# Block-sorted attention with a mixture of experts behind it: weights asked for in GpSimd's order, denominators by products of their own, an exchange on three queues

## The chip, the core and the metric

The kernel runs on one core of one Trainium2 chip. The core has five engines with instruction streams of their own: TensorE (PE; its weight loads stand as PEld), VectorE (DVE), ScalarE (ACT), GpSimd (POOL) and SyncE (SP). They share an on-chip memory, SBUF, of 128 partitions, and TensorE writes its results to PSUM, in banks of 128 partitions by 2 KB. Sixteen DMA engines move data between the chip's main memory and SBUF; an engine's stream asks for such a transfer and goes on. Streams wait for each other by semaphores. The metric is the device time in microseconds (us) of one execution; the data before is the median of three.

## The reference, cut to what matters

`P` is a small matrix for each of 4 batches and 8 heads, made near doubly stochastic by five rounds of row and column normalisation (Sinkhorn). It mixes the 8 blocks (96 rows of 64) of keys and of values; then each block of queries attends to its sorted block. The result, 3072 rows of 512, goes through 8 experts that are all computed for all rows and summed with weights from a second, longer Sinkhorn.

```python
for _ in range(5):
    P = np.exp(P - np.max(P, axis=-1, keepdims=True))
    P = P / (np.sum(P, axis=-1, keepdims=True) + 1e-09)
    P = P / (np.sum(P, axis=-2, keepdims=True) + 1e-09)
k_sorted = np.einsum('bhij,bhjcd->bhicd', P, k_b)   # v_sorted likewise
scores = scale * np.matmul(q_b, k_sb.transpose(0, 1, 2, 4, 3))
attn = np.exp(scores - max); attn /= attn.sum(-1)
x = np.matmul(attn, v_sb)                           # -> [3072, 512]
# P: 8 rounds of normalisation of exp(x @ w_gate)
for e in range(8):
    out += P[:, e:e+1] * (np.maximum(x @ w1[e], 0) @ w2[e])
```

## The kernel before, in words

**The whole.** Batch 0's attention runs alone (line numbers are the profile's, L1 is the first line of the kernel file). Batches 1, 2 and 3 follow, each woven with the first expert's products for the batch before it (`expert0`, L299 and L306), so that TensorE always has expert products to put between the short ones of the attention. Then come the other experts, about three quarters of the time, which the change does not touch. TensorE's and GpSimd's instructions are pinned to the order in which the program writes them (`pin`); those of the other engines are ordered by a scheduler unless pinned.

**The loads.** GpSimd asks for all loads from main memory (`load_rest` L75, `load_w1` L84, `load_w2` L89), since they turn 4-byte into 2-byte numbers on the way. It asks first for the gate's weights `wg` (L96), then for the queries, values and keys of batch 0 in halves of four heads, then for batch 1's values.

**Start of batch 0.** ScalarE and VectorE compute the Sinkhorn of `P` on 32 partitions (L111 to L124). `Prep` repeats it 16 times (L128), eight products spread it over the partitions (L352), VectorE copies the result to `Pb` (L354) and builds from `Pb` and a mask the block matrices `R` (`build_r`, L140), with which a single product sorts the values of a head (L152) or the keys (L196).

**Values and the exchange.** `sort_values` makes eight products, one a head; VectorE and ScalarE copy them by turns into `vs` (L154). There the 96 rows of a sorted block lie in 16 partitions, 6 to each. The mix needs them in 96 partitions. Eight DMAs, the exchange, carry block for block from `vs` to `vsb` (L161), by turns from SyncE and GpSimd. To each value row a column of ones is appended, so that the mix's 65th column is the softmax's denominator.

**Batch 0's attention.** Its plan is a string, each letter a step with its pair of heads: `q` turns the queries (TensorE L174, ScalarE copy L186), `k` sorts the keys (L196, VectorE copy L201), `s` makes scores (L215) and their exponentials on ScalarE (L222) into `atp`; `m` mixes: products of the exponentials with `vsb` (L232), two banks a head, the reciprocal of the 65th column (L235) and the product with it (L236), both on VectorE; `t` turns the result (L243) and copies it to `xtT` (L246, on ScalarE in batch 0); `l` makes the gate's logits from it (L257); `v` sorts two heads of batch 1's values, and its last call issues batch 1's exchange; `w` makes products that nobody reads (`warm`, L344, 512 columns each). The plan of batch 0 before:

```python
plan = ("k0 k1 w4 s0 q2 k2 w2 s1 q3 k3 w3 s2 w4 s3 w3 m0 w3 m1 t0 v0 w3 m2 t1 v0 w3 "
        "m3 t2 v0 v0 w3 t3 l0 w3 l3 v0" if first else
```

Seven PSUM banks go round among all these steps.

**The probe.** The first expert's weights are wanted only behind batch 0's attention. GpSimd copies two numbers of `vsb` (`held`, L362), which it can do only once the exchange has landed, and `issue_after` lets the requests for w1, w2 and batch 1's keys and queries follow that copy.

**Behind batch 0.** Twelve steps of `expert0` come first (8 of four products with w1, L299, then 4 half steps with w2, L306), then batch 1's attention, woven with the rest. It begins with the queries of both first pairs, for which the first halves of batch 1's queries must have landed; the third pair needs the second half.

Of the kernel before, what the change touches and what calls it, by code (L numbers as in the profile page):

```python
# [13 lines left out]
F32 = mybir.dt.float32  # L14
# [11 lines left out]
def kernel(  # L26
# [66 lines left out]
    make_identity(nc, Ibig)  # L93
    load_batch(0, [(x, l0, 4) for l0 in (0, 4) for x in "qvk"])
    wg = ones.tile([128, 4, E], BF16)
    nc.gpsimd.dma_start(out=wg, in_=moe_w_gate.rearrange("(kk k) e -> k kk e", k=128))  # L96
    load_batch(1, [("v", 0, 8)])
    mask16 = ones.tile([128, 16], F32)
# [5 lines left out]
    vsbt = [perp.tile([128, VW], BF16, name=f"vsb{n}") for n in range(2)]  # L104
    vs = vsp.tile([128, 6, 8, 65], BF16)
    nc.vector.memset(vs[:, :, :, 64:65], 1.0)

# [18 lines left out]
    Prep = perp.tile([32, 8, 8, 16], BF16)  # L126
    for eng, i0 in ((nc.vector.tensor_copy, 0), (nc.scalar.copy, 4)):
        eng(Prep[:, i0:i0 + 4], mkap(P, [P.ap[0], [8, 4], [1, 8], [0, 16]], off=i0 * 8))  # L128

# [4 lines left out]
    Rt = {}  # L134

    def build_r(bb, eng, n):

        Rt[bb] = perp.tile([128, 8, 8, 16], BF16, name=f"R{bb % 2}")
        for h in range(0, 8, n):
            ins = eng.tensor_tensor(  # L140
                out=mkap(Rt[bb], [Rt[bb].ap[0], [16, 8 * n], [1, 16]], off=h * 128),
                in0=mkap(Pb, [Pb.ap[0], [1, 8 * n], [0, 16]], off=(bb * 8 + h) * 8),
                in1=mkap(mask16, [mask16.ap[0], [0, 8 * n], [1, 16]]),
                op=ALU.mult)
            if eng is nc.gpsimd:
                pin(ins)


    def sort_values(bb, bank):
        for h in range(8):  # L150
            vps = bank([128, 384], F32)
            pin(nc.tensor.matmul(vps, Rt[bb][:, h].rearrange("p i c -> p (i c)"),  # L152
                                 vt[bb][:, h, :], start=True, stop=True))
            (nc.vector.tensor_copy if bb == 0 and h % 2 else nc.scalar.copy)(  # L154
                vs[:, :, h, 0:64], vps.rearrange("p (kk d) -> p kk d", d=64))
            if h % 2:
                yield

        for i in range(NB):
            eng = nc.gpsimd if i % 2 else nc.sync  # L160
            (pin if bb == 0 else lambda ins: ins)(eng.dma_start(  # L161
                out=mkap(vsbt[bb % 2], [[VW, 96], [1, 520]], off=i * 520),
                in_=vs[16 * i:16 * i + 16].rearrange("p kk h d -> p kk (h d)")))
# [43 lines left out]
    def scores(bb, hp, bank):  # L207

        for b in range(2):
# [10 lines left out]
            for h in range(2):  # L220
                at[bb, hp, h, b] = sp.tile([128, 4, 96], BF16, name="atp", bufs=ATP)
                nc.scalar.activation(out=at[bb, hp, h, b][0:96], in_=sps[h][0:96],  # L222
                                     func=AF.Exp, scale=scale)

    def mix(bb, hp, h, bank):
        if h == 0:
            og[bb, hp] = sp.tile([128, NB, 2, 64], BF16, name="og", bufs=2)
        for b in range(2):
            ops = bank([128, 4, 65], F32)
# [33 lines left out]
    def attention(bb, bank, values=None, warm=None):  # L263
        first = bb == 0

        def step(what, hp):
            if what == "q":
                queries(bb, hp, bank)
            elif what == "k":
                keys(bb, hp, bank)  # L270
            elif what == "s":
                scores(bb, hp, bank)
            elif what == "t":
                turn(bb, hp, bank, nc.scalar.copy if first else nc.vector.tensor_copy)
            elif what == "l":
                logits(bb, bank, (0, 1, 2) if hp == 0 else (3,))
            elif what == "v":
                next(values, 0)
            elif what == "w":
                warm(hp)  # L280
            else:
# [53 lines left out]
    with tc.tile_pool(name="ps0", bufs=7, space=bass.MemoryType.PSUM,  # L335
# [15 lines left out]
        for i in range(8):  # L351
            pin(nc.tensor.matmul(pbps[:, i, :], Prep[:, i].rearrange("p j c -> p (j c)"),  # L352
                                 Ibig[0:32, 0:32], start=True, stop=True))
        nc.vector.tensor_copy(Pb, pbps.rearrange("p i g -> p g i"))  # L354
# [25 lines left out]
    with ExitStack() as c2:  # L380
# [4 lines left out]
        for bb in range(1, B):  # L385
            ex = expert0(bb - 1, lambda: mps.tile([128, 8, 384], BF16, name="hTs"),
                         ebank, ebank, pin)
            at1, left = attention(bb, bank1), 16 if bb == 1 else 26
            for _ in range(28 - left):
                next(ex)  # L390
            last = 3 if bb + 1 < B else 0
            left -= last
            cut = lambda k: left * k // 12
            weave(at1, ex, 5, cut(5))
            if bb + 1 < B:
                load_batch(bb + 1, [(x, 0, 8) for x in "vkq"])
                build_r(bb + 1, nc.gpsimd, 4)
            else:
# [413 lines left out]
```

## Time and profile before

| What | us |
|---|---|
| median of 3 runs (range) | 680.86 (680.52 to 681.43) |
| profiled execution | 680.97 |
| its span | 679.2 |
| TensorE busy in the span | 659.0 |
| DMA moved | 36.58 MB, mean 54 GB/s |

The span is from the first to the last instruction of the profile; the profiled execution's own time is 1.8 us longer. A row of the timeline or of the groups reads: start, length, engine, line, operation, output `<-` inputs, shapes, how many; in brackets the idle time of the engine before it and what ended it. A matmul's shape is that of its stationary operand, then of its moving one. Neighbouring instructions of one kind are merged into one row, so that a row of 16 products holds one latency and 15 steps. A row of DMA issues reads: output `<-` input, the queue that asked (SPq, POOLq), how many, KB of each, and us from issue to landing (the median). Queue rows read: packets, MB, and the time they took as a share of 16 engines (q0 holds GpSimd's transfers, q1 SyncE's); packets overlap, so that a share can pass 100%. A row by stretches reads: from:to, length, then each engine's busy time and count (PE, PEld, DVE, ACT, POOL), the granted TensorE clock, the DMA share and GB/s.

### The profile page before, as it was taken

How to read it: one execution, taken by the hardware profiler on the slowest of the kernel's cores; microseconds unless marked ns; L12 is line 12 of the kernel's file. 1: busy time of each engine (PE TensorE's matmuls, PEld its weight loads, DVE VectorE, ACT ScalarE, POOL GpSimd, SP SyncE). 2: the span in 40 equal slices, each digit the busy share in tenths (PEclk: the TensorE clock that was granted, in tenths of full speed). 3: DMA queues.
4: the chain of work that ended last, by engine and by line, in shares of the span. 5: the costliest groups of instructions: out<-in, count | busy, mean ns of one | idle time of the engine just before them, and what ended most of it. 6: DMA issues, size and time to landing. Idle time of an engine off the chain costs nothing.

```text
span 679.2 us, 13352 instructions
## 1 busy us (share of the span) xinstructions
PE 659.0 (97%) x5136; PEld 434.1 (64%) x5136; DVE 474.8 (70%) x977; ACT 380.5 (56%) x737; POOL 473.6 (70%) x439
## 2 busy tenths in 40 slices
PE   4989999999999999999999999999999999999997
PEld 2656666554566666666666666666666666666665
DVE  6727556758587777777777777777777777777775
ACT  3757646356767765455555555555555555555540
POOL 4542324474979998959697988879796979836641
PEclk9999999999999999999999999999999999999999
DMA  9898843402140304030403030020303040000224
GB/s 146 168 217 127 139 82 63 63 1 37 28 62 2 63 1 63 1 63 1 63 1 63 1 50 14 12 52 3 61 1 63 1 63 1 1 0 32 94 84 167
DMA packets 31905, 36.58 MB, mean 54 GB/s; under 512 B 2016, under 2 KB 24288, under 8 KB 31840
## 3 DMA queue, kind: packets, MB, share of 16 engines
q0 software_dynamic: 26400, 27.82, 25.8%
q1 hardware_dynamic: 5440, 7.90, 3.4%
q8 instruction: 40, 0.66, 0.4%
q14 instruction: 25, 0.20, 0.1%
HBM read 52.45 MB, written 6.29 MB: 86 GB/s over the span
## 4 chain that ended last, share of the span: by engine, by line
PE 88%; DVE 5%; DMA 4%; issue 1%; ACT 1%; POOL 1%; SPq 0%; DVEq 0%; POOLq 0%
PE oacc L635 36%; PE bk L524 36%; PE bank L299 4%; PE bank L306 3%; DMA qt<-in_q_dram 3%; PE bank L232 1%; PE bk L601 1%; PE oacc L700 1%; PE bk L692 1%; DMA vsb<-vs 1%; PE bank L215 1%; PE bank L196 1%; PE bank L243 1%; DVE xc L460 1%; PE bk L700 1%
## 5 line engine op out<-in xcount | busy, mean ns | idle before, releaser
L585 DVE SCALAR_TENSOR_TENSOR osbl<-oacc,glog,osbl 128x256 f32<-128x256 f32 (+1 forms) x410 | 219.4, 536 | 127.7 <-PE oacc L635 117.8
L510 ACT ACTIVATE hT<-bk 128x512 bf16<-128x512 f32 (+1 forms) x176 | 104.2, 592 | 151.8 <-PE bk L524 131.9
L524 PE MATMUL bk<-xtT,w1e 128*128 128x512 bf16 x504 | 149.1, 379 | 0.0
L635 PEld LDWEIGHTS <-hs 128*128 128x128 bf16 x984 | 96.3, 98 | 63.0 <-issue 0.3
L635 PEld LDWEIGHTS <-hT 128*128 128x128 bf16 x904 | 88.4, 98 | 59.6 <-issue 2.4
L625 POOL TENSOR_TENSOR hs<-hT 128x512 bf16<-128x512 bf16 x82 | 94.7, 1155 | 38.3 <-DVE hT L513 28.6
L635 PE MATMUL oacc<-w2e,hT 128*128 128x256 bf16 x764 | 114.6, 273 | 1.1 <-DVE osbl L585 1.1
L625 POOL TENSOR_TENSOR hs<-hT,hs 128x512 bf16<-128x512 bf16 x82 | 95.1, 1159 | 6.4
L625 POOL TENSOR_TENSOR hs<-hs,hT 128x512 bf16<-128x512 bf16 x82 | 95.1, 1159 | 6.4
L524 PE MATMUL bk<-xc,wc 128*128 128x512 bf16 x336 | 99.1, 379 | 0.0
L635 PE MATMUL oacc<-w2e,hs 128*128 128x256 bf16 x616 | 92.4, 273 | 0.0
L524 PEld LDWEIGHTS <-w1e 128*128 128x128 bf16 x672 | 65.7, 98 | 14.9 <-issue 3.6
L559 ACT COPY p<-bk 128x512 f32<-128x512 f32 x84 | 49.1, 585 | 23.9 <-PE bk L524 23.8
L513 DVE CUSTOM_DVE_ANT_0 hT<-bk,p 128x512 bf16<-128x512 f32 x84 | 57.9, 690 | 6.6 <-PE bk L524 1.9
L553 ACT COPY u<-bk 128x512 f32<-128x512 f32 x84 | 49.2, 586 | 22.2 <-PE bk L524 22.1
L544 ACT COPY bk<-bk 128x512 f32<-128x512 f32 x84 | 48.0, 571 | 20.5 <-PE bk L524 20.5
L513 DVE CUSTOM_DVE_ANT_0 hT<-bk,u 128x512 bf16<-128x512 f32 x84 | 57.2, 681 | 0.6 <-PE bk L524 0.6
L635 PE MATMUL oacc<-w2s,hs 128*128 128x256 bf16 x368 | 55.2, 273 | 0.0
L578 DVE SCALAR_TENSOR_TENSOR s<-bk,hT 128x512 bf16<-128x512 f32 x80 | 54.5, 681 | 0.0
L524 PEld LDWEIGHTS <-wc 128*128 128x128 bf16 x504 | 49.4, 99 | 7.5
L524 PE MATMUL bk<-xc,w1e 128*128 128x512 bf16 x168 | 49.9, 379 | 1.9 <-DVE hT L513 1.8
L524 PE MATMUL bk<-xtT,wc 128*128 128x512 bf16 x168 | 50.0, 379 | 0.0
(129 smaller groups left out, 858.5 us busy)
## 6 DMA issues: line engine op xcount, KB each, us to landing
w1e<-in_moe_w_dram POOLq DMA_DIRECT2D x8, 1024.0 KB, 8.1
w2e<-in_moe_w_dram POOLq DMA_DIRECT2D x8, 1024.0 KB, 8.9
out_dram<-osbl SPq DMA_DIRECT2D x23, 256.0 KB, 2.0
vt<-in_v_dram POOLq DMA_DIRECT2D x3, 768.0 KB, 10.5
vsb<-vs SPq DMA_DIRECT2D x16, 97.5 KB, 4.8
vsb<-vs POOLq DMA_DIRECT2D x16, 97.5 KB, 4.4
qt<-in_q_dram POOLq DMA_DIRECT2D x4, 384.0 KB, 12.8
kt<-in_k_dram POOLq DMA_DIRECT2D x4, 384.0 KB, 13.3
```

The source lines that it names most:

```text
L299: hold(nc.tensor.matmul(hps[:, 0:n], w1t[e][:, kk, fb * 128:(fb + 1) * 128], xtT[:, kk, c0:c0 + n], start=(kk == 0), stop=(kk == 3)))
L306: hold(nc.tensor.matmul(oacc, hTs[:, fb, tt * 128:(tt + 1) * 128], w2t[e][:, fb, :], start=(fb == 0), stop=(fb == 7)))
L510: relu = lambda o, x: nc.scalar.activation(out=o, in_=x, func=AF.Relu)
L513: return nc.vector._custom_dve(TENSOR_ADD_SAT, out=o, in0=x, in1=y, s0=TOP, s1=0.0)
L524: pin(nc.tensor.matmul(ps, wa[:, kk, :], xa[:, kk, :], start=(first and kk == 0), stop=(kk == 1), skip_group_check=True))
L544: pin(nc.scalar.copy(t["w"], t["u"]))
L553: pin(nc.scalar.copy(t["u2"], t["u"]))
L559: pin(nc.scalar.copy(t["p5"], t["v"]))
L578: pin(nc.vector.scalar_tensor_tensor(out=s3[:, i, :], in0=t["w"], scalar=0.0, in1=c12, op0=ALU.max, op1=ALU.subtract))
L585: pin(nc.vector.scalar_tensor_tensor(out=o, in0=ps, scalar=glog[:, t, e:e + 1], in1=o, op0=ALU.mult, op1=ALU.add))
L625: pin(nc.gpsimd.tensor_tensor(out=s[:, c], in0=a, in1=b, op=o))
L635: pin(nc.tensor.matmul(ps, h[:, fb, :], w[:, fb, :], start=(first and fb == 0), stop=(fb == 3), skip_group_check=True))
```

## The change

What is done, part by part:

- The request for `wg` moves behind batch 1's values and is pinned there, so the loads of batch 0 are asked for first.
- `Prep` is split 5 and 3 between VectorE and ScalarE instead of 4 and 4.
- Batch 0's `R` is built by VectorE straight from the PSUM bank; `Pb` is copied by ScalarE, and its user is GpSimd's `R` of the later batches.
- Of batch 0's value copies VectorE makes those of heads 3, 5 and 7 and ScalarE the other five.
- Batch 0's exchange goes by turns from SyncE, GpSimd and ScalarE instead of SyncE and GpSimd.
- The probe copy is gone. GpSimd, behind its exchange pieces, builds half of batch 1's `R`, asks for w1, builds the other half, asks for w2 and then for batch 1's keys and queries.
- A new step `d` computes batch 0's softmax denominators by 16 products of the exponentials with a column of ones, for a pair of heads, and one reciprocal. The mix of batch 0 then has 64 columns, all eight blocks of a head in one bank, and one VectorE product of 512 elements a partition.
- The last turn's copy of batch 0 moves to VectorE.
- Heads 4 to 7 of batch 1's values, and its exchange, move from batch 0's plan to the first expert steps (`late`).
- The unread products are fewer in all (23 instead of 31) and placed anew.

```diff
     load_batch(0, [(x, l0, 4) for l0 in (0, 4) for x in "qvk"])
+    load_batch(1, [("v", 0, 8)])
     wg = ones.tile([128, 4, E], BF16)
-    nc.gpsimd.dma_start(out=wg, in_=moe_w_gate.rearrange("(kk k) e -> k kk e", k=128))
-    load_batch(1, [("v", 0, 8)])
+    pin(nc.gpsimd.dma_start(out=wg, in_=moe_w_gate.rearrange("(kk k) e -> k kk e", k=128)))
...
+    one = pp.tile([128, 1], BF16)
+    nc.vector.memset(one, 1.0)
...
-    for eng, i0 in ((nc.vector.tensor_copy, 0), (nc.scalar.copy, 4)):
-        eng(Prep[:, i0:i0 + 4], mkap(P, [P.ap[0], [8, 4], [1, 8], [0, 16]], off=i0 * 8))
+    for eng, i0, n in ((nc.vector.tensor_copy, 0, 5), (nc.scalar.copy, 5, 3)):
+        eng(Prep[:, i0:i0 + n], mkap(P, [P.ap[0], [8, n], [1, 8], [0, 16]], off=i0 * 8))
...
-    def sort_values(bb, bank):
-        for h in range(8):
+    def sort_values(bb, bank, n=8, h0=0):
+        for h in range(h0, n):
...
-            (nc.vector.tensor_copy if bb == 0 and h % 2 else nc.scalar.copy)(
+            (nc.vector.tensor_copy if bb == 0 and h in (3, 5, 7) else nc.scalar.copy)(
...
-        for i in range(NB):
-            eng = nc.gpsimd if i % 2 else nc.sync
+        for i in range(NB if n == 8 else 0):
+            eng = ((nc.sync, nc.gpsimd, nc.scalar)[i % 3] if bb == 0 else
+                   nc.gpsimd if i % 2 else nc.sync)
...
+    def denominators(hp, bank):
+
+        dps = bank([128, 2, NB], F32)
+        for h in range(2):
+            for i in range(NB):
+                pin(nc.tensor.matmul(dps[0:96, h, i:i + 1], at[0, hp, h, i // 4][0:96, i % 4, :],
+                                     one[0:96], start=True, stop=True))
+        den[hp] = pp.tile([128, 2, NB], F32, name=f"den{hp}")
+        nc.vector.reciprocal(out=den[hp][0:96], in_=dps[0:96])
...
+        if bb == 0:
+            ops = bank([128, NB, 64], F32)
+            for i in range(NB):
+                a = (i * 8 + 2 * hp + h) * 65
+                pin(nc.tensor.matmul(ops[0:96, i], at[bb, hp, h, i // 4][0:96, i % 4, :],
+                                     vsbt[0][0:96, a:a + 64], start=True, stop=True))
+            nc.vector.tensor_mul(og[bb, hp][0:96, :, h, :], ops[0:96],
+                                 mkap(den[hp], [[den[hp].ap[0][0], 96], [1, NB], [0, 64]],
+                                      off=h * NB))
+            return
...
-                turn(bb, hp, bank, nc.scalar.copy if first else nc.vector.tensor_copy)
+                turn(bb, hp, bank, nc.scalar.copy if first and hp < 3 else nc.vector.tensor_copy)
...
-        plan = ("k0 k1 w4 s0 q2 k2 w2 s1 q3 k3 w3 s2 w4 s3 w3 m0 w3 m1 t0 v0 w3 m2 t1 v0 w3 "
-                "m3 t2 v0 v0 w3 t3 l0 w3 l3 v0" if first else
+        plan = ("k0 k1 w3 s0 q2 k2 w2 s1 q3 k3 d0 w1 s2 w2 d1 s3 w7 m0 d2 w1 m1 t0 w2 m2 t1 v0 "
+                "d3 m3 t2 w2 v0 t3 l0 w3 l3" if first else
...
-        nc.vector.tensor_copy(Pb, pbps.rearrange("p i g -> p g i"))
-        build_r(0, nc.vector, 2)
+        Rt[0] = perp.tile([128, 8, 8, 16], BF16, name="R0")
+        for h in range(0, 8, 2):
+            nc.vector.tensor_tensor(
+                out=Rt[0][:, h:h + 2],
+                in0=mkap(pbps, [pbps.ap[0], [1, 2], [32, 8], [0, 16]], off=h),
+                in1=mkap(mask16, [mask16.ap[0], [0, 2], [0, 8], [1, 16]]), op=ALU.mult)
...
-        build_r(1, nc.gpsimd, 4)
-
-        held = pp.tile([96, 2], BF16)
-        gate = nc.gpsimd.tensor_copy(
-            held, mkap(vsbt[0], [[VW, 96], [520, 2]], off=6 * 520 + 519))
-        with tc.issue_after(gate.ins):
-            load_w1(0)
-            load_w2(0)
-            load_rest(1, [(x, l0, 4) for l0 in (0, 4) for x in "kq"])
-        for _ in attention(0, bank0, sort_values(1, bank0), warm):
+        nc.scalar.copy(Pb, pbps.rearrange("p i g -> p g i"))
+        half = build_r(1, nc.gpsimd, 4)
+        next(half)
+        load_w1(0)
+        next(half, 0)
+        load_w2(0)
+        load_rest(1, [(x, l0, 4) for l0 in (0, 4) for x in "kq"])
+        for _ in attention(0, bank0, sort_values(1, bank0, 4), warm):
...
+            late = sort_values(1, bank1, 8, 4) if bb == 1 else iter(())
             for _ in range(28 - left):
                 next(ex)
+                next(late, 0)
```

More of the change, by code (lines that the diff above doesn't have):

```diff
@@ L146, in build_r @@
                 pin(ins)
-    def sort_values(bb, bank):
-        for h in range(8):
+            yield
+    def sort_values(bb, bank, n=8, h0=0):
+        for h in range(h0, n):
             vps = bank([128, 384], F32)
@@ L223, in scores @@
                                      func=AF.Exp, scale=scale)
+    den = {}
+    def denominators(hp, bank):
[6 more added lines that the diff above has]
+        nc.vector.reciprocal(out=den[hp][0:96], in_=dps[0:96])
     def mix(bb, hp, h, bank):
@@ L280, in step @@
                 warm(hp)
+            elif what == "d":
+                denominators(hp, bank)
             else:
@@ L396 @@
                 load_batch(bb + 1, [(x, 0, 8) for x in "vkq"])
-                build_r(bb + 1, nc.gpsimd, 4)
+                for _ in build_r(bb + 1, nc.gpsimd, 4):
+                    pass
             else:
```

## The prediction

> **What bounds the kernel now.** I began with the page's first part and the chain of work that ended last: the profiled execution is TensorE work almost from end to end, so a change counts only where TensorE waits or is kept from starting.
>
> ```profile
> PE 659.0 (97%) x5136; PEld 434.1 (64%) x5136; DVE 474.8 (70%) x977; ACT 380.5 (56%) x737; POOL 473.6 (70%) x439
> PE 88%; DVE 5%; DMA 4%; issue 1%; ACT 1%; POOL 1%; SPq 0%; DVEq 0%; POOLq 0%
> ```
>
> Next the same chain piece by piece, up to 49 us (start, length, what), because the change touches only that part:
>
> ```profile
> 19.57 4.87 DMA vsb<-vs
> 25.06 0.83 POOL w1e L84
> 28.98 19.76 DMA qt<-in_q_dram
> 48.78 0.53 PE bank L174 x12
> ```
>
> The reader is to see a chain without TensorE: the sorted values of batch 0 set off the exchange, the exchange lands at 24.44 (19.57 + 4.87), GpSimd's probe copy then lets w1 be asked for at 25.06, and behind w1 and w2 stand the keys and queries of batch 1, whose last piece lands at 48.74. From there the chain is TensorE's. So TensorE's timeline up to that point decides (the bracket is the wait before the row):
>
> ```profile
> 18.48 0.56 PE L215 MATMUL bank<-qTs,kTs 64*96 64x96 bf16 x16 [0.44 <-DVE kTs L201]
> 23.06 1.04 PE L344 MATMUL unread<-Ibig 128*128 128x512 bf16 x4
> 24.52 0.82 PE L344 MATMUL unread<-Ibig 128*128 128x512 bf16 x3
> 25.18 0.69 PE L232 MATMUL bank<-vsb,atp 96*96 96x65 bf16 x12
> 26.14 0.33 PE L232 MATMUL bank<-vsb,atp 96*96 96x65 bf16 x4 [0.28 <-ACT atp L222]
> 35.35 0.31 PE L257 MATMUL bank<-wg,xtT 128*128 128x8 bf16 x6 [0.40 <-ACT xtT L246]
> 35.52 5.36 PE L299 MATMUL bank<-xtT,w1e 128*128 128x384 bf16 x32
> 44.73 0.86 PE L174 MATMUL bank<-Ibig,qt 128*64 128x128 bf16 x24 [0.40 <-DMA qt<-in_q_dram]
> 48.78 0.53 PE L174 MATMUL bank<-Ibig,qt 128*64 128x128 bf16 x12 [0.95 <-DMA qt<-in_q_dram]
> ```
>
> The first mix (25.18) comes straight from unread products and after the landing at 24.44: it waits for its turn, not for the exchange. The loads cost TensorE 0.40 + 0.95 = **1.35 us** of waiting at 44.73 and 48.78. And if TensorE came there sooner, it would only wait longer: the earlier request and the shorter stretch need each other.
>
> **The change, part by part.**
>
> *Front, up to the first scores.* Vector work sets it:
>
> ```profile
> 13.72 0.42 DVE L354 COPY Pb<-bank 128x256 f32<-128x256 f32 x1 [0.55 <-PE bank L352]
> 14.18 1.43 DVE L140 TENSOR_TENSOR R<-Pb,mask 128x256 bf16<-128x256 f32 x4
> 15.53 1.95 DVE L154 CAST vs<-bank 128x384 bf16<-128x384 f32 x4
> 15.04 1.63 ACT L154 CAST vs<-bank 128x384 bf16<-128x384 f32 x4 [0.98 <-PE bank L152]
> 18.89 1.62 ACT L222 ACTIVATE atp<-bank 96x384 bf16<-96x384 f32 x4 [2.23 <-PE bank L215]
> 25.61 1.62 ACT L222 ACTIVATE atp<-bank 96x384 bf16<-96x384 f32 x4 [0.65 <-PE bank L232]
> ```
>
> R0 is now built from the bank itself, so the 0.46 us from 13.72 to 14.18 go; I let its four products keep their 0.36 us each though they now read a bank (a copy from a bank, Pb's, took 0.42 for the same elements: at most 0.25 more in all). VectorE has three value copies instead of four (1.95 / 4 = 0.49 less), ScalarE five: 1.63 / 4 = 0.41 more, from about 14.95 to 17.0. VectorE then ends at 13.72 + 1.43 + 0.1 + 3 x 0.49 = 16.8 instead of 17.48, the keys of heads 0 and 1 follow, and the scores start at about 17.87: **-0.6**. The unread products before them fall from 4 to 3, 0.22 us (1.04 - 0.82), so TensorE is there in time. The exchange starts when ScalarE is through, about 17.1 instead of 17.57. The other split of Prep (5 and 3 rows) moves 0.1 us from one engine to the other at 12.75, and the memset of ones falls in VectorE's idle start, where it has nothing to do before 2.5: both nothing.
>
> *Denominators ahead of the mixes.* Between the first scores and the first mix stand 12 unread products before (2, 3, 4, 3) and 12 after (2, 1, 2, 7), and new are d0 and d1 with 16 products of one column each. No such product is in the trace. Nearest are the logits' (8 columns, 18 in 0.60) and the mix's own (65 columns, 16 in 0.71 on the chain; the row is batch 1's):
>
> ```profile
> 52.44 0.71 PE bank L232 x16
> ...
> L257 PE MATMUL bank<-wg,xtT 128*128 128x8 bf16 x72 | 2.7, 167 | 0.4 <-ACT xtT L246 0.4
> ...
> 33.69 0.60 PE L257 MATMUL bank<-wg,xtT 128*128 128x8 bf16 x18
> 32.05 0.81 PE L152 MATMUL bank<-vt,R 128*128 128x384 bf16 x4
> 30.02 0.49 PE L152 MATMUL bank<-vt,R 128*128 128x384 bf16 x2
> ```
>
> A group's length holds one product's latency (0.167 for the logits' by the view of groups), so the step is (0.60 - 0.167) / 17 = 0.0255, and 16 steps are about 0.42; the bounds are 0.4 and 0.71, and I take 0.42, since the column count decides and 1 is nearest to 8. Two of them: **+0.85** (at most +1.4). So TensorE reaches the first mix at 25.18 - 0.6 + 0.85 = 25.4.
>
> *First mix to first expert product.* Before, this is 25.18 to 35.52, 10.34 us. By steps: four mixes 2.84, four turns 1.2, values 8 x 0.16 (half of 0.81 - 0.49) = 1.3, 15 unread 3.3, logits 0.65: 9.3, plus the two waits of 0.28 and 0.40 above. After: mixes 2.8, turns 1.2, two value steps (4 products) 0.65, 8 unread (1, 2, 2, 3) 1.75, d2 and d3 0.85, logits 0.65: 7.9. The 0.28 goes, as a head's mix now takes one bank instead of two; the 0.40 goes, since the last turn's copy leaves ScalarE. VectorE must follow:
>
> ```profile
> 27.44 0.24 DVE L235 RECIPROCAL recips<-bank 96x4 f32<-96x4 f32 x2
> 27.64 0.75 DVE L236 TENSOR_TENSOR og<-bank,recips 96x256 bf16<-96x256 f32 x2
> 32.49 0.75 DVE L236 TENSOR_TENSOR og<-bank,recips 96x256 bf16<-96x256 f32 x2
> 34.44 0.85 ACT L246 COPY xtT<-bank 128x768 bf16<-128x768 bf16 x1
> ```
>
> Before, the last three pairs of heads take it from 27.44 to 33.24, 1.93 us a pair, as long as TensorE's step there. After, it is two products of 512 elements (each at most the 0.75 of two of 256) and one reciprocal of about 0.17: 1.7 at most, off the path. I allow 0.6 for waits that stay where before had about 1.0 (10.34 - 9.3), so 8.5: **-1.8** (bounds -0.9, with d at the mix's price and waits of 1.0, and -2.4, with none). The first expert product starts at 33.95.
>
> *Values of batch 1.* Heads 4 to 7 (4 x 0.16 = 0.65) go behind the first expert steps: **+0.65**, paid here and taken out above. Their four ScalarE copies lie beside expert products. Their exchange goes out at about 36.5, three expert steps in; its user, the first mix of batch 1, is on the chain at 52.44, some 50 after, and even a piece that takes the 14.2 us of batch 1's first on GpSimd's queue (row below) lands at 50.7: at worst half a us late, and less, since the loads ahead of it end 4 us sooner.
>
> *w1 in GpSimd's order.* GpSimd's rows, with the landing times of the issues (last number, us):
>
> ```profile
> 17.57 2.60 SPq L161 DMA_DIRECT2D vsb<-vs  x4
> 18.17 2.11 POOL L161 DMA_DIRECT2D vsb<-vs  x4 [10.26 <-issue]
> 20.27 2.10 POOL L140 TENSOR_TENSOR R<-Pb,mask 128x512 bf16<-128x512 f32 x2
> 39.75 0.51 POOL L161 DMA_DIRECT2D vsb<-vs  x1 [3.25 <-DMA w2e<-in_moe_w_dram]
> w1e<-in_moe_w_dram POOLq DMA_DIRECT2D x1, 1024.0 KB, 8.1
> vsb<-vs POOLq DMA_DIRECT2D x1, 97.5 KB, 14.2
> 27.50:40.00 12.50, 12.11 (x144) 8.20 (x142) 5.72 (x26) 9.02 (x18) 4.12 (x8) 1.00 1.17 198
> ```
>
> GpSimd's first piece went 0.6 behind the exchange's start, so after: three pieces from 17.7 at 0.53 end at 19.3, half of R1 (1.05) at 20.35, w1 at about 20.65: 4.4 earlier. From 27.5 on, the last row, the DMA moves 198 GB/s without a gap, so all behind w1 follows: the two query pieces land at about 40.3 and 44.4 where 44.7 and 48.74 stood. TensorE wants them at 44.33 - 0.9 = 43.4 (by the sum so far) and 3.1 us later, 46.5. They are there, with 2 us to spare: **-1.35**. w1, wanted at 33.95, lands at 28.8. Waits added: GpSimd's 22nd DMA waited for its 14th (39.75, w2). If each waits for the one eight before it, w1, now the 12th, waits for the 4th, a load of batch 0, w2 and the first keys for the next two, and the other queries and keys for v1, wg and the first exchange piece, which should have landed by 22.5, while w2's turn comes at 22.6 and theirs behind it. wg itself moves behind v1 on this queue: its issue lies in GpSimd's idle 10.26 before 18.17, and its user is the logits near 32. Without it in front, the loads of batch 0 are asked for sooner by its issue, to no use but that v1 is out of the exchange's way sooner.
>
> *The third queue.* ScalarE now issues two exchange pieces (0.5 to 0.7 each by SyncE's and GpSimd's) once the last value copy is done, from 17.1 to 18.3, and behind them stand the Pb copy, 0.42, which GpSimd's R1 needs at 19.3, and the first exponentials, due at 18.3. They lie in the idle 2.23 before 18.89; the worst is the copy's 0.42, and ScalarE stood idle 0.65 before its last exponentials at 25.61. I count nothing. [...]
>
> **Sum.** At the second query piece: -0.6 + 0.85 - 1.8 + 0.65 - 1.35 = -2.25. Behind it TensorE waits for no DMA, so the gain stays. The profiled execution took 680.97 (span 679.2), so 678.7; the median of the runs shown is 680.86, 0.1 less: **678.6**.
>
> **Rivals.** *The exchange lands late and the mixes wait: slower.* Without the probe, w1 may flow while pieces are still out. For it: batch 1's piece on GpSimd's queue took 14.2 us amid loads. With that from 17.7, the landing is 31.9, the first mix 6.5 late, the time 685. It decides from a landing at 27.65 (25.4 + 2.25). Against: the 14.2 went behind w2, keys and queries, these go ahead of w1, behind what before's had to pass in 4.9 us. Chance 0.07.
>
> *They share by turns.* Batch 1's pieces beside the load stream show a share per queue in 41 to 42 us:
>
> ```profile
> q0 software_dynamic: 163, 0.12, 77.1%
> q1 hardware_dynamic: 143, 0.12, 46.7%
> ```
>
> 0.12 MB a us for SyncE's pieces (q1): from w1's request at 20.65, the five pieces of 97.5 KB that SyncE and ScalarE issue would take 4.1 us at that rate, so 24.8, in time; with v1's remainder in front, some 26: 0.6 late, 679.2. [...] Chance 0.08.
>
> *The stretch does not shrink.* With d at 0.71 throughout (+1.15) the query pieces are still in time, but TensorE comes to them about 1.15 later: 679.8, inside 0.2%. It needs the stationary loads, not the columns, to set the step; the logits' row speaks against. Chance 0.13.
>
> *The loads gain nothing.* If w1's request moves less than 1 us (a wait on GpSimd for Pb or a landing), TensorE is early and waits for queries at about 47.8: 679.9. Chance 0.1.
>
> **How the numbers follow.** The forecast has 0.62, the four rivals 0.38. A change under 0.2% (1.4 us) is what a measurement can hardly tell from none. Faster: the forecast, the turns and a part of the third and fourth, 0.76; same 0.16; slower 0.08. The range: below, the stretch at -2.4 and a further 0.7 in the front, 677.3; above, the third and fourth rival and some of the exchange's lateness, 680.5.
>
> **What would show it.** Right: first scores near 17.9; w1 asked for near 20.7; first mix near 25.4 with no wait for vsb; 16 denominators in 0.4 to 0.5; first expert product near 34; no wait for qt at batch 1's queries, and TensorE's second query step near 46.5. Wrong: a wait for vsb ahead of the mixes, ScalarE late with exponentials, a qt wait that stays, or a stretch from mix to expert over 9.5 us.

## The result, and the profile after

| | before | after |
|---|---|---|
| median (range, runs) | 681.08 us (680.52 to 681.43, 10) | 678.71 us (677.63 to 680.59, 10) |
| profiled execution | 680.97 | 678.37 |
| its span | 679.2 | 676.6 |

The ratio is 0.9967, with a 95% interval of 0.9959 to 0.9976: 2.4 us or 0.33% faster. The forecast was 678.6, with 677.3 to 680.5 as its range. The runs of the new kernel lie further apart than those of the old one, 3.0 us against 0.9.

First the profile's page of the new kernel, its engines and its chain of waits:

```profile
PE 660.5 (98%) x5192; PEld 436.7 (65%) x5192; DVE 473.0 (70%) x957; ACT 380.0 (56%) x738; POOL 473.5 (70%) x437
PE 94%; DVE 4%; ACT 1%; issue 1%; DMA 0%; DVEq 0%
```

The chain's 4% of DMA are gone, and TensorE has 94% of it instead of 88%. TensorE's timeline of the new kernel (start, length, what; a bracket would show a wait):

```profile
17.09 0.56 PE L219 MATMUL bank<-qTs,kTs 64*96 64x96 bf16 x16
...
20.34 0.88 PE L236 MATMUL bank<-one,atp 96*96 96x1 bf16 x16
...
25.10 0.87 PE L248 MATMUL bank<-vsb,atp 96*96 96x64 bf16 x16
...
33.81 0.81 PE L327 MATMUL bank<-xtT,w1e 128*128 128x384 bf16 x4
34.46 0.49 PE L155 MATMUL bank<-vt,R 128*128 128x384 bf16 x2
...
43.20 0.86 PE L178 MATMUL bank<-Ibig,qt 128*64 128x128 bf16 x24
...
46.24 0.53 PE L178 MATMUL bank<-Ibig,qt 128*64 128x128 bf16 x12
```

No row from the first scores (17.09) to the second query step (46.24) has a bracket: the waits for queries (0.40 and 0.95), for `xtT` and for `atp` have gone, and none for `vsb` has come. The second query step stood at 48.78, so it is 2.54 earlier, and the profiled execution is 2.60 shorter: nearly all of the gain of this pair of profiles is made before 46 us, as forecast. GpSimd's timeline, and the landing times of batch 1's query pieces (the tile's view):

```profile
16.77 1.61 POOL L165 DMA_DIRECT2D vsb<-vs  x3 [9.03 <-ACT Pb L391]
18.37 1.09 POOL L142 TENSOR_TENSOR R<-Pb,mask 128x512 bf16<-128x512 f32 x1
19.38 0.83 POOL L84 DMA_DIRECT2D w1e<-in_moe_w_dram  x1
...
24.40 0.78 POOL L75 DMA_DIRECT2D qt<-in_q_dram  x1
```

```profile
DMA to landing us min/median/max: 15.3/17.0/21.1
```

w1 is asked for at 19.38 instead of 25.06. The second query piece, asked for at 24.40, lands at 45.5 (the maximum, 21.1), 0.7 before it is wanted. That is less room than the 2 us of the prediction.

### The profile page after: what moved, and what is told of

Its sections match the earlier page's. It is cut to its first block, busy times and chain, and to the rows that moved or that the text cites. A ratio compares the mean times of both kernels' runs of the same rounds, so it can differ in the third digit from the quotient of the medians.

```text
span 676.6 us, 13435 instructions
## 1 busy us (share of the span) xinstructions
PE 660.5 (98%) x5192; PEld 436.7 (65%) x5192; DVE 473.0 (70%) x957; ACT 380.0 (56%) x738; POOL 473.5 (70%) x437
## 4 chain that ended last, share of the span: by engine, by line
PE 94%; DVE 4%; ACT 1%; issue 1%; DMA 0%; DVEq 0%
PE bk L557 37%; PE oacc L668 37%; PE bank L327 5%; PE bank L334 4%; PE bank L258 1%; PE bank L219 1%; PE bk L634 1%; PE bank L200 1%; PE unread L372 1%; PE oacc L733 1%; PE bk L725 1%; PE bank L155 1%; PE bank L269 1%; PE oacc L725 1%; DVE xc L493 1%
```

## The experiments

Each is compared with the kernel before, run along with it on the same chip. That kernel's median was 681.08 in the result above and 681.00, 681.38 or 681.43 in the experiments, so two experiments are best compared by their ratios. In the profiles I use two marks: **S**, the start of the last column product of `P`'s Sinkhorn, which no edit touches, and **q2**, TensorE's second query step of batch 1. VectorE's rows for S, before and after:

```profile
12.46 0.26 DVE L124 TENSOR_TENSOR P<-P,cs 32x64 f32<-32x64 f32 x1
```

```profile
11.73 0.26 DVE L126 TENSOR_TENSOR P<-P,cs 32x64 f32<-32x64 f32 x1
```

S was 12.00 to 12.10 in all the other kernels, those with `wg` in front included, so the two profiles of the result are the extremes: late before, early after. It moves the whole front by up to 0.7 us from one profile to another, so q2 - S is the fairer measure of one profile. It was 36.32 before and 34.51 after.

### The early request alone, and all but the early request

`early_w1_alone`, on the kernel before:

```diff
-        build_r(1, nc.gpsimd, 4)
-        held = pp.tile([96, 2], BF16)
-        gate = nc.gpsimd.tensor_copy(held, ...)
-        with tc.issue_after(gate.ins):
-            load_w1(0)
-            load_w2(0)
-            load_rest(1, ...)
+        half = build_r(1, nc.gpsimd, 4)
+        next(half)
+        load_w1(0)
+        next(half, 0)
+        load_w2(0)
+        load_rest(1, ...)
```

> The kernel before without its probe: w1 behind the exchange pieces and half of R1 on GpSimd, nothing else. First theory: w1 is asked for at about 21.7 instead of 25.06, the two waits for batch 1's queries (0.40 and 0.95) go and nothing else moves: 1.35 less, 679.7. Rival: w1's transfer holds up the exchange, which lands at 26 or later, and the first mix waits: no gain or a loss, 681 to 682.

`after_probe`, on the kernel after: the same hunk the other way round, all else as changed.

> The changed kernel with the probe put back. First theory: the exchange lands at about 24.1, w1 is asked for near 24.7 instead of 19.38, the second query piece lands near 48.4 where TensorE wants it at 46.3 and, behind a first wait, 47.2: two waits together of 1.8 to 2.2, 680.4. Rival: the early request is not needed once the rest is in place, the time stays within 0.5 of the changed kernel's 678.7.

The early request alone: **678.45 us** (678.32 to 678.95, 5 runs), ratio 0.9961 (0.9948 to 0.9975). All but the early request: **681.03** (679.82 to 682.02, 11 runs), ratio 0.9995 (0.9986 to 1.0004). The timeline of the first kernel, GpSimd's row and then TensorE's, and below it that of the second:

```profile
20.80 0.83 POOL L84 DMA_DIRECT2D w1e<-in_moe_w_dram  x1
...
46.84 0.53 PE L175 MATMUL bank<-Ibig,qt 128*64 128x128 bf16 x12
```

```profile
24.06 0.18 POOL L395 COPY held<-vsb 96x2 bf16<-96x2 bf16 x1 [3.24 <-DMA vsb<-vs]
24.55 0.83 POOL L84 DMA_DIRECT2D w1e<-in_moe_w_dram  x1 [0.30 <-issue]
...
48.39 0.53 PE L178 MATMUL bank<-Ibig,qt 128*64 128x128 bf16 x12 [1.62 <-DMA qt<-in_q_dram]
```

The request alone gives the whole gain that can be measured, and all else without it gives none. Without the probe, q2 comes 1.48 earlier by q2 - S (34.84), against the 1.35 of the prediction. The time is 1.2 us below the 679.7 that was expected, so the two waits are not all of it: of the 2.62 between the profiled executions (680.97 and 678.35), 1.48 is q2 - S, 0.46 an earlier S, and 0.68 lies behind q2, where a chance of timing decides (see "Behind q2" below). With the probe, the shorter stretch only lets TensorE come sooner to queries that are not there: the two waits of 0.40 and 0.95 become one of 1.62, and q2 - S stays at 36.29. The prediction said that this would happen. It also said that the two parts "need each other", and that holds one way only: the stretch needs the request, the request needs nothing.

The second kernel also shows the exchange by itself: the probe runs at 24.06, when the last piece is there. With w1 under way beside it, the first mix at 25.10 does not wait. The rivals of a late exchange are refuted.

### Without the denominators' products

`after_no_den`: batch 0 mixes again with 65 columns and the reciprocals of before; the plan keeps all else.

```diff
-        if bb == 0:
+        if False:
             ops = bank([128, NB, 64], F32)
...
-        plan = ("... q3 k3 d0 w1 s2 w2 d1 s3 w7 m0 d2 w1 m1 t0 w2 m2 t1 v0 d3 m3 t2 ..."
+        plan = ("... q3 k3 w1 s2 w2 s3 w7 m0 w1 m1 t0 w2 m2 t1 v0 m3 t2 ..."
```

> The changed kernel without the denominators' products: the d steps are taken out of the plan, batch 0 mixes with 65 columns and two banks a head and takes its reciprocals as before; the unread products stay as in the changed kernel. First theory: TensorE is spared 4 x 0.69 = 2.8 us, but the first mix can come no sooner than the exchange (24.1), and VectorE then needs 1.93 us a pair of heads again: the first expert product at 33.3 to 33.9 against 33.81, so the denominators' products are worth nothing or cost 0.5: 678.2 to 678.8. Rival, the prediction's: they shorten the stretch to the first expert product, and without them it is 1 us or more longer: 679.7 or more.

**677.83** (677.44 to 679.85, 5 runs), ratio 0.9954 (0.994 to 0.9967): the median is 0.9 below the changed kernel's, though the two intervals overlap, and q2 - S is 34.00 instead of 34.51. By the profile, step `d` costs more than it saves, and TensorE's timeline of this kernel shows where:

```profile
24.68 0.69 PE L258 MATMUL bank<-vsb,atp 96*96 96x65 bf16 x12
...
29.27 1.40 PE L258 MATMUL bank<-vsb,atp 96*96 96x65 bf16 x16
...
33.66 0.81 PE L327 MATMUL bank<-xtT,w1e 128*128 128x384 bf16 x4
```

Its first mix is at 12.58 from S (12.10 here), where the kernel after has 13.37: `d0` and `d1` with the products around them cost 0.79, about half of what they take by themselves, because without them the scores wait for ScalarE's exponentials (the third pair's scores take 1.02 until the next row, where the kernel before takes 0.59). From there to the first expert product it takes 8.98 against 8.71: `d2` and `d3` are paid for by mixes that wait less, with 0.27 left. The four mixes take 2.85 from their own start to the next row's in the kernel after and 3.92 here, 1.23 of it the mix at 29.27. The stretch shrinks from 10.34 without `d` almost as well as with it, by the fewer unread products and the values moved behind.

### A wider stationary operand

`after_wide_den`, on the kernel after: three in four of `d`'s products load 128 columns of the exponentials (the last 32 belong to the next block; their results fall in partitions 96 to 127 and are not read).

```diff
+                j = i % 4
+                n = 128 if j < 3 else 96
+                a = at[0, hp, h, i // 4].rearrange("p j c -> p (j c)")
-                pin(nc.tensor.matmul(dps[0:96, h, i:i + 1], at[0, hp, h, i // 4][0:96, i % 4, :],
+                pin(nc.tensor.matmul(dps[0:n, h, i:i + 1], a[0:96, 96 * j:96 * j + n],
                                      one[0:96], start=True, stop=True))
```

> The changed kernel with the denominators' stationary operands 128 columns wide where the tile has them (three blocks of four; the 32 extra columns are the next block's and their results are not read). First theory: what sets the 0.043 us step of these products is loading 96 columns, and a load of 128 goes faster, 0.026 as in the logits: a d step takes 0.5 instead of 0.69, 0.7 to 0.8 less in four, and the first expert product is 0.5 to 0.8 sooner. Rival: the step is set by something else (the rows, the semaphores) and stays at 0.043 or grows with the columns; the time stays.

**678.35** (677.26 to 680.12, 6 runs), ratio 0.996 (0.9948 to 0.9972). TensorE's timeline of this kernel:

```profile
22.55 0.63 PE L239 MATMUL bank<-one,atp 96*128 96x1 bf16 x16
```

The same 16 products take 0.63 instead of 0.88, although they load more. So it is the load of 96 columns that sets the step of `d`, not the one column that moves. The stretch from first mix to first expert product falls with it, from 8.71 to 8.26; ahead of the first mix nothing is gained (8.06 from the first scores instead of 8.01). The median's 0.36 is within the spread of both kernels. This profiled execution, 679.08, stood idle 1.90 ahead of `Prep`, and its clock was halved from 13 to 17 us (0.74, 0.50, 0.50 and 0.56 by the microsecond), so its front can't be compared.

### The gate's weights: moved alone, and put back

`wg_alone`, on the kernel before:

```diff
-    wg = ones.tile([128, 4, E], BF16)
-    nc.gpsimd.dma_start(out=wg, in_=...)
     load_batch(1, [("v", 0, 8)])
+    wg = ones.tile([128, 4, E], BF16)
+    pin(nc.gpsimd.dma_start(out=wg, in_=...))
```

> The kernel before with wg's request alone moved behind batch 1's values. First theory, from the two traces: with wg in front the vector engine's Sinkhorn reaches its last column product 0.72 us later (12.75 against 12.03), and that lead goes through the exchange and the probe to batch 1's queries, so the first values are sorted some 0.7 us sooner, w1 is asked for 0.5 to 0.8 sooner and the time falls by 0.4 to 0.8, to about 680.4. Rival, the prediction's: the move is of no use, within 0.2 us of before, and Prep stays at 12.75.

`after_wg_first`, on the kernel after: the same hunk the other way round.

> The changed kernel with wg's request back in front of the loads. First theory: TensorE's first burst then starts 1 us later and runs up to Prep as in the kernel before, the clock stays whole, and nothing else depends on the loads of batch 0: 678.0 to 678.4 with a spread of about 1 us. Rival: the sooner loads carry part of the gain (the exchange has to wait for batch 1's values on the same DMA engines), and without them the time is 679.0 or more.

Moved alone: **681.4** (680.18 to 682.35, 11 runs), ratio 1.0 (0.9991 to 1.0009). Put back: **679.39** (678.45 to 679.6, 5 runs), ratio 0.9969 (0.9958 to 0.9981). TensorE's timeline of the kernel with `wg` in front again:

```profile
15.36 0.81 PE L155 MATMUL bank<-vt,R 128*128 128x384 bf16 x4 [0.41 <-DMA vt<-in_v_dram]
```

The second half of batch 0's values is late there by 0.41, and q2 - S is 35.05, so by the profile the move is worth 0.54 in the changed kernel; the ratios, 0.9969 and 0.9967, are too wide to show it. Moved alone it gave nothing in the median, and its profile by stretches says why (the column after POOL's is the granted clock):

```profile
14.00:15.00 1.00, 0.99 (x5) 0.33 (x4) 1.00 (x4) 0.19 (x1) 0.00 (x0) 0.69 1.32 205
15.00:16.00 1.00, 1.00 (x5) 0.48 (x4) 0.95 (x3) 0.77 (x2) 0.00 (x0) 0.50 1.31 201
16.00:17.00 1.00, 1.00 (x6) 0.21 (x5) 0.89 (x2) 0.75 (x2) 0.00 (x0) 0.50 1.32 205
17.00:18.00 1.00, 1.00 (x25) 1.00 (x24) 0.95 (x2) 0.21 (x1) 0.00 (x0) 0.61 1.31 204
```

The sooner loads let TensorE finish its early unread products sooner, it then stands idle 1.43 before `Prep`, and its clock is halved from 14 to 18 us: what the four rows lack to full speed, 0.31 + 0.50 + 0.50 + 0.39, is 1.7 us of full-speed work. That would lower the mean granted clock of an execution, which is on record for each run, by 1.7 / 680 = 0.0025. Six of the eleven runs have a mean clock of 0.996 or 0.997 and a median of 681.6; the other five have 0.998 to 1.000 and a median of 680.4, 0.6 below the kernel before. So the move was worth about 0.6 where the clock stayed whole, near the 680.4 that was expected, though not by the lead of S that the expectation builds on: with `wg` in front S was 12.00 and 12.04 in two other kernels, against 12.10 here.

### More and fewer unread products

`after_warm13` and `after_warm4`, on the kernel after, only change how many unread products stand ahead of `Prep`:

```diff
-        warm(9)
+        warm(13)
```

> The changed kernel with 13 unread products instead of 9 ahead of the Sinkhorn's spreading products. First theory: asking for the loads sooner makes TensorE's first burst end up to 1.5 us before Prep is there, and in some executions its clock then halves for some 4 us (0.50 from 15 to 17 us in the run with wg's move alone); four more products fill the gap, so the slow executions go: the spread of the times falls from 3.0 us to about 1 and the median to 677.8 to 678.3. Rival: the spread has another cause (the subtractions on the vector engine near 113 us, or the exchange), and spread and median stay at 678.7 within 0.3.

> The changed kernel with 4 unread products instead of 9 ahead of the Sinkhorn's spreading products, so that TensorE stands idle some 1.1 us longer before them. First theory (the clock): TensorE's first burst is then too short or its gap too long, the clock is at half for several us between 13 and 18 us in most executions, and the time rises by 1 to 2, to 679.7 or more. Rival: the unread products there cost nothing and bring nothing, 678.7 within 0.4.

Thirteen: **678.75** (678.09 to 680.3, 5 runs), ratio 0.9967 (0.9955 to 0.9979), which misses the lower median that was expected. Four: **680.37** (679.72 to 682.79, 12 runs), ratio 0.9986 (0.9977 to 0.9994). TensorE's timeline with four:

```profile
12.93 0.39 PE L380 MATMUL bank<-Ibig,Prep 32*128 32x32 bf16 x8 [3.17 <-DVE Prep L130]
...
14.93 2.77 PE L155 MATMUL bank<-vt,R 128*128 128x384 bf16 x8
```

After 3.17 us of idleness the eight sorting products take 2.77, where the kernel after takes 1.60, and q2 - S rises from 34.51 to 36.38; by the ratios the time rises by 1.3 us. So the unread products do matter, and the slower products in the front, 2.77 for 1.60, cost 1.3 to 1.9. The clock column does not show them: it reads 1.00 from 13 to 18 us in this profile, and only the lengths of the products tell. Why thirteen did not help, its own profiled execution (680.3) shows by stretches, at another place:

```profile
121.00:122.00 1.00, 1.00 (x5) 0.53 (x4) 1.00 (x2) 0.89 (x3) 1.00 (x2) 0.55 0.00 0
122.00:123.00 1.00, 1.00 (x10) 0.73 (x8) 0.10 (x1) 0.29 (x1) 1.00 (x1) 0.50 0.00 0
123.00:124.00 1.00, 1.00 (x16) 1.00 (x15) 0.85 (x4) 0.20 (x1) 1.00 (x4) 0.50 0.00 0
124.00:125.00 1.00, 1.00 (x12) 0.78 (x10) 1.00 (x6) 0.00 (x0) 0.27 (x1) 0.74 0.02 3
```

Here the clock is halved behind short waits of TensorE for VectorE, near 118 to 120 us (0.52, 0.34 and 0.30): again 0.45 + 0.50 + 0.50 + 0.26 = 1.7. The kernel after has the same waits there (0.53, 0.34 and 0.31) with its clock whole. The next but one experiment looks at these waits.

### Two queues for the exchange

`after_two_queues`, on the kernel after:

```diff
-            eng = ((nc.sync, nc.gpsimd, nc.scalar)[i % 3] if bb == 0 else
-                   nc.gpsimd if i % 2 else nc.sync)
+            eng = nc.gpsimd if i % 2 else nc.sync
```

> The changed kernel with its exchange on SyncE and GpSimd alone. First theory: with three queues SyncE's third issue took 1.62 us, since the pieces ahead cannot move until batch 1's values are through at about 19.5; with two the landing is the same within 0.5 us of 24.1, the first mix (25.1) does not wait, w1 is asked for 0.5 later, and the time is the same within 0.4. Rival: the third queue is needed; the exchange lands 1 us later, past the first mix, and the time is 679.5 or more.

**679.54** (677.92 to 682.33, 10 runs), ratio 0.9976 (0.9962 to 0.9989). The interval overlaps the changed kernel's, the first mix does not wait, and q2 - S is 34.49 against 34.51. The third queue is worth nothing on the path up to there. The median lies where the rival put it (679.5 or more), but not for the rival's reason: four of the ten runs have a mean clock of 0.994 to 0.996 and a median of 681.4, the other six a median of 678.5. The times are too wide to say more.

### Two versions that take the best of it

`best1` is the kernel after without `d`, with thirteen unread products and with the wide operand (128 columns) in the mixes of all batches. `best2` adds one line, which takes some VectorE work near 115 us to GpSimd:

```diff
-    for _ in sum_x(0, nc.vector, lambda ins: ins):
+    for _ in sum_x(0, nc.gpsimd):
         pass
```

> The changed kernel without the denominators' products, with 13 unread products at the start, and with the stationary operand of three of four mixes widened to 128 columns in all batches (results of the extra 32 columns are not read). First theory: where TensorE sets the pace (batches 1 to 3, 12 mix steps of 16 products), a step falls from 0.71 to about 0.54, so 2.0 less than without the denominators: 675.5 to 676.3. Rival: the mixes of batches 1 to 3 lie beside VectorE's reciprocals and products, which then set the pace: 677.3 or more.

> The kernel of best1 with the first differences of x taken from VectorE to GpSimd, since in the traces VectorE's four subtractions at 113 to 122 us take up to 1.64 each beside GpSimd's and 0.68 alone, and TensorE waits 1.2 there. First theory: these waits go, and with them the halved clock at 121 to 125 us that one run showed: 1 to 2 less than best1. Rival: GpSimd, which must then make them ahead of the sums of the second expert's weights, becomes late, and the expert products wait for it: 1 us or more longer than best1.

`best1`: **676.69** (675.79 to 676.97, 5 runs), ratio 0.993 (0.9918 to 0.9941), just above the 675.5 to 676.3 that was expected. `best2`: **674.4** (674.36 to 674.57, 4 runs), ratio 0.9897 (0.9883 to 0.9912), the fastest version found, 1.0% below the kernel before. TensorE's timeline of `best1`:

```profile
49.68 0.71 PE L260 MATMUL bank<-vsb,atp 96*128 96x65 bf16 x16
...
115.45 0.81 PE L329 MATMUL bank<-xtT,w1e 128*128 128x384 bf16 x4
117.00 0.20 PE L219 MATMUL bank<-qTs,kTs 64*96 64x96 bf16 x1 [0.73 <-DVE osbl L344]
117.54 0.57 PE L219 MATMUL bank<-qTs,kTs 64*96 64x96 bf16 x8 [0.34 <-DVE og L264]
118.42 0.38 PE L219 MATMUL bank<-qTs,kTs 64*96 64x96 bf16 x7 [0.30 <-DVE og L264]
118.75 1.47 PE L329 MATMUL bank<-xtT,w1e 128*128 128x384 bf16 x8
```

A group of 16 mixes takes 0.71 instead of 0.87. The waits at 117 come from VectorE, which is held up by the first three of the four subtractions of `sum_x`. In the kernel before, VectorE's and GpSimd's timelines show what happens to them:

```profile
118.57 1.64 DVE L460 TENSOR_TENSOR xtT<-xtT 128x1024 bf16<-128x1024 bf16 x1
...
123.55 0.68 DVE L460 TENSOR_TENSOR xc<-xtT,xc 128x1024 bf16<-128x1024 bf16 x1
```

```profile
118.06 1.60 POOL L332 TENSOR_TENSOR wc<-w1e,wc 128x512 bf16<-128x512 bf16 x1
...
122.41 1.15 POOL L332 TENSOR_TENSOR w1e<-w1e 128x512 bf16<-128x512 bf16 x1
123.52 1.72 POOL L332 TENSOR_TENSOR wc<-w1e,wc 128x512 bf16<-128x512 bf16 x1
```

Beside GpSimd's subtraction one of VectorE's takes 1.64, and GpSimd's takes 1.60 beside it and 1.15 otherwise. VectorE's of 0.68 is not one that ran alone, as the expectation has it: it lies within GpSimd's of 1.72, which here bears the whole delay. None of VectorE's four ran alone in this profile. In `best2` GpSimd does both kinds one after another, its eight on `w1e` take 1.14 to 1.16 each, and TensorE's timeline has no wait there:

```profile
115.46 0.81 PE L329 MATMUL bank<-xtT,w1e 128*128 128x384 bf16 x4
116.21 0.56 PE L219 MATMUL bank<-qTs,kTs 64*96 64x96 bf16 x16
116.70 1.47 PE L329 MATMUL bank<-xtT,w1e 128*128 128x384 bf16 x8
```

The two kernels are level up to these scores (q2 at 46.19 and 46.20, the products ahead of the scores at 115.45 and 115.46), and behind them `best1` goes on at 118.75, `best2` at 116.70. So 2.05 of the 2.1 us between their profiled executions (676.66 and 674.57) lie in this one group of scores: 1.37 are its three waits for VectorE, the rest goes with doing it in three pieces instead of one. The four runs of `best2` lie within 0.2 us.

## Why the prediction was right, point by point

**The mechanism.** "w1 in GpSimd's order" was the term that carried the gain. The two query waits, -1.35, went entirely, and the two experiments on the request show that it is the cause. Asked for at 19.38 instead of the forecast 20.65, w1 landed 10.8 later, at 30.2, not at 28.8; the second query piece landed at 45.5, not at 44.4. Both were in time. The order of the load stream was judged rightly, its speed too well by 1 to 2.5 us.

**The sum**, term by term, up to q2:

| term | predicted | measured | from |
|---|---|---|---|
| first scores | -0.6 | -1.39 | 18.48 to 17.09 |
| from there to the first mix (`d0`, `d1`) | +0.85 | +1.31 | 6.70 to 8.01 |
| first mix to first expert product | -1.8 | -1.63 | 10.34 to 8.71 |
| values behind the expert steps | +0.65 | +0.65 | two times 0.32 |
| query waits | -1.35 | -1.35 | none left |
| sum | -2.25 | -2.54 | 48.78 to 46.24 |

The measured terms make -2.41, and -0.13 lies in small steps between them. Two terms were off, and they cancelled in part. There is luck in how near the sum came: 0.73 of the measured -2.54 is the earlier S, which no term forecast, and counted from S the kernel gained 1.81, not 2.25. The split was wrong too: the parts other than the request add 0.33 to what the request gives alone (34.84 and 34.51), where the sum gave them 0.9.

**The step that was mis-sized: the denominators.** "I take 0.42, since the column count decides and 1 is nearest to 8" was wrong. The chain of the new kernel, piece by piece:

```profile
22.48 0.68 PE bank L236 x16
...
25.97 0.69 PE bank L236 x16
```

Sixteen products take 0.68 to 0.69, a step of 0.043, and the whole group is as long as the mix's own. That is the upper bound of the prediction (0.71), taken from the row with the same stationary operand of 96 columns. The logits' row was near in moved columns and far in the stationary ones: it loads 128. With 128 columns here too, `d` came to 0.63 a group by the timeline, between the two. The third rival, that the stationary loads set the step, was therefore right in its cause. Its time (679.8) did not come: of its 1.15 only 0.63 arrived (0.46 ahead of the mixes and 0.17 behind), the rest was taken up by the 0.6 allowed for waits that TensorE did not have, and the earlier S gave 0.73 back. That `d0` and `d1` were put at 0.85 and cost 0.79 when taken out is chance: they took twice 0.74 to 0.77 up to the next row, and filled waits for ScalarE that the forecast had not counted.

**The front.** Counted from S, the first scores came at 6.02 before and 5.36 after: -0.66, for a forecast of -0.6 from the edits. VectorE's and ScalarE's timelines of the kernel after bear its parts out:

```profile
12.96 1.42 DVE L384 TENSOR_TENSOR R<-bank,mask 128x256 bf16<-128x256 f32 x4 [0.46 <-PE bank L380]
14.59 1.49 DVE L157 CAST vs<-bank 128x384 bf16<-128x384 f32 x3 [0.20 <-PE bank L155]
```

```profile
14.10 2.01 ACT L157 CAST vs<-bank 128x384 bf16<-128x384 f32 x5 [0.87 <-PE bank L155]
15.96 0.43 ACT L391 COPY Pb<-bank 128x256 f32<-128x256 f32 x1
```

The four products from the bank keep their 0.36 each, and the value copies take what they took before. The other 0.73 is S itself, 12.46 against 11.73. VectorE's rows make it up of three: the load of `P` landed 0.22 sooner, one operation on the column sums (`cs`, at 4.30 before and 4.08 after) took 0.16 instead of 0.48, and the reduction that makes the mask cost the chain 0.20 before and nothing after. Only the last goes with an edit: the mask is made later in all three kernels with `wg` in front. The other two no edit touches: S was 12.10 in `after_no_den` and `after_two_queues`, which have the front of the kernel after, so most of the 0.73 is the luck of this pair of profiles.

**"To no use" of the move of `wg`** was wrong by the profiles. Put back, it costs 0.54 up to q2, where the second half of the values is then late by 0.41. By itself it brings nothing in the median, since six of its eleven runs have a mean clock of 0.996 or 0.997 and a median of 681.6.

**The exchange and the third queue** were counted as nothing, and so they were. The tile's view of `vsb` in the kernel after:

```profile
L165 SPq DMA_DIRECT2D vsb<-vs x3: 690/1020/1624, 16.2 to 18.0; - x3
L165 POOL DMA_DIRECT2D vsb<-vs x3: 534/548/557, 16.8 to 17.8; - x3
L165 ACTq DMA_DIRECT2D vsb<-vs x2: 610/636/662, 16.2 to 16.9; - x2
```

All issues start by 18.0, and with at most 6.8 to landing the last is there by 24.8 at the latest, before the mix at 25.10. The issuing order on ScalarE was not the forecast's (its `Pb` copy ran ahead of the pieces, not behind), which cost nothing either.

**Behind q2** the prediction kept the gain unchanged. The profiled times less q2 are 632.19 before and 632.13 after, so this held. It was less sure than it looked: the same difference is 631.5 for the early request alone and 631.4 with the probe. All of that lies in the one group of scores near 118 us shown above for `best1`. From the start of the expert products ahead of it to the row behind it, the group takes 3.04 before, 3.09 after, and 2.40 and 2.39 in those two. It goes with the first of VectorE's subtractions, which takes 1.32, 1.37, 0.67 and 0.67, by how it falls beside GpSimd's. Other profiles fit: 1.15 and 2.88 in `wg_alone`, 1.00 and 2.72 in `after_no_den`. So the profile of the early request alone came off 0.7 better here than that of the whole change, by a timing that no part of the prediction looked at.

**What stays open** is the wider spread of the changed kernel. Two causes were seen in single profiles, the halved clock (at 13 to 18 or at 121 to 125 us, 1.7 each time) and the subtractions' overlap (up to 0.7). The mean clock of each run speaks for the first: three of the ten runs of the result have 0.996 or 0.997, with a median of 680.5, the other seven 678.4. Sorted so, after the fact, the split is no test, and where in these runs the clock was halved was not seen. Thirteen unread products did not lower the median, and one of their five runs still had the halved clock. That `best2` is narrow speaks for the stretch near 115 us.

## What to carry to other kernels

When a load stream stands behind a probe of another transfer, ask for the stream in the issuing engine's own order and check only that the other transfer still lands in time: here that alone gave as much as the whole change, and what shortened the compute gave nothing measurable until it was done. Price a small product by the row that has the same stationary width (sixteen of `d` took 0.68 to 0.69; the mix's row, of that width, gave 0.71, the logits' 0.42), and where an operand has 96 columns, try 128 (here 0.63 for 0.88 in `d`, 0.71 for 0.87 in the mixes). Where two engines subtract in SBUF side by side, look at the lengths of both, since either may bear the delay (VectorE took 1.64 in one place, GpSimd 1.72 instead of 1.15 in another), and at which engine's delay the critical engine waits for, before deciding who does what.

## What the runs showed of the hardware that was not expected

- **The clock halved behind some gaps and not behind others.** It was halved in `wg_alone` and `after_wide_den` after idle times of 1.43 and 1.90 ahead of `Prep`, and in `after_warm13` after scattered waits of 0.52, 0.34 and 0.30. Each time the four rows lack 1.7 us of full speed, that is 3.4 us at half speed. A gap between the first two left the clock at 1.00 (`after_probe` stood idle 1.50 and sorted in 1.60), so what decides is not shown. The column also missed a slowing: with four unread products it read 1.00 while the sorting took 2.77.
- **The wider load was the quicker one.** 96 columns took a step of 0.043 us and a mix group 0.87; with 128 columns in three of four products the mix group took 0.71.
- **SyncE's DMA issues stretched.** Its three pieces took 0.69, 1.02 and 1.62 us to issue while GpSimd's took 0.55 each. Their queue, q1, moved one packet before 19.5, though the first was asked for at 16.2 and batch 1's values, asked for at 6.1, were still landing (14.2 after that request). In this kernel nothing waited for it.
